# w_out on 128 and 32 lanes, row sums of two quarters, and a transposing lane maximum in a decode kernel of attention and gMLP

## The chip, the cores and the metric

The kernel runs on one core of one Trainium2 chip. The metric is the device time of one execution in microseconds, as the median of several runs. Every time below comes from these runs or from one profiled execution of the kernel before.

## The reference

One decode step (one token for each of four batch rows, D = 640) through two blocks that share a layer-normalized input. All inputs and the output are bfloat16.

```python
xn = layernorm(x)                                    # (4, 1, 640)
# A: 32 heads, Dh = 128, 4096 cached keys and values per batch row and head
q = (xn @ wq) per head
p = softmax(q . k_cache * 128**-0.5)                 # over the 4096 keys
a = (p . v_cache) @ wo                               # (4096, 640)
# B: gMLP, F = 1728, Fh = 864
z = gelu(xn @ w_in)
z1, z2 = z[..., :Fh], layernorm(z[..., Fh:])
g = w_sp * z2 + b_sp                                 # one token: two scalars
b = (z1 * g) @ w_out                                 # (864, 640)
out = x + a + b
```

k_cache and v_cache have 134 MB each; with wq, wo, w_in and w_out the kernel reads 282 MB from HBM.

## The kernel before

**Units.** The work goes by NU = 16 units: a unit is eight heads of one batch row (`hg, b = divmod(u, 4)`; HG = 4 groups of heads). Its keys, 8 MB, lie on 128 lanes, 16 lanes a head and 256 keys a lane, and are cut into NK = 4 quarters of 64 keys. The 64 quarters of all units are the steps `n` of the main loop (L708).

**A step.** `product` (L514, VectorE) multiplies the quarter by the query, which is broadcast to the lanes in `qbc`. `fold_half` (L520, VectorE) adds the upper half of the 128 columns to the lower. `sums` (L529, TensorE) adds the 64 columns that are left in eight groups of 8 by eight matmuls with the identity, into a PSUM tile `s_ps` of 64 x 8. `row_sums` (L542, VectorE) of the step before adds those eight into the scores `s_sb`.

**The end of a unit**, in the first step of the next one. `head_max` takes the maximum over a lane's 256 scores (L551), then over the 16 lanes of a head: a 32 x 32 transpose of that maximum, broadcast (L553), a mask `far` added (L556), a maximum with negation (L558). `exps` (L564, ScalarE) forms the exponentials and `by_head` (L575, VectorE) spreads them over the columns of their heads in one of two halves of the tile `p_m`. `stage_q` (L496, L504) makes `qbc` of the next unit.

**V.** In the second step of the next unit (`turns`, L697; the last units differ) `weighted` (L599) multiplies all of V by `p_m` with 64 matmuls into `pv`. `take` (L611, ScalarE) copies the result out and `pick_unit` (L630) collects it by head in `o_ps`.

**A group's turn.** After four units, in the first step of the unit after that (n = 20, 36, 52), `group_turn` divides by the denominators `den` (L640, L646), transposes (L655) and adds (L660), and `group_proj` (L668) multiplies by wo into `out_ps`. The matmul of `den` (`group_den`, L615) stands earlier, at the turn three steps before, ahead of `weighted`. The last group goes another way (L757 to L788): V of the last unit lies in the ring and is multiplied in pieces (L778) as they land.

**Order.** From L702 on the order on TensorE, VectorE, ScalarE and SP is the one written. The loads go out on SP's queue in the order of `loads` (L177). `pump` issues them as long as the place that the next one needs isn't in `busy`; K has a ring of seven quarters, V one place (`v_all`), and wo lies in a slot of the ring (`WO_AT`). A slot is given free as soon as its `sums`, its `weighted` or its `group_proj` are issued, and the DMA waits for their end.

**gMLP.** `gmlp` (L372) is a generator whose parts are run in steps 0 to 2. Its 864 columns are six chunks of 128 lanes and four of 24 (`NFF`, `FR`, `FT`): 100 matmuls form `zT` (L380), VectorE and ScalarE do gelu and layernorm, and 20 matmuls (L480) multiply by w_out. w_out lies in three parts: rows of six to a lane, of which five are in `v_all` and the sixth in the tile `p_m` (L118 to L121, by SP), and the last 96 rows on 24 lanes, also in `p_m`, by five transfers of five or four lanes each, issued by ScalarE (L115).

Of the kernel before, what the change touches and what calls it, by code (L numbers as in the profile page):

```python
# [9 lines left out]
FP32 = mybir.dt.float32  # L10
BF16 = mybir.dt.bfloat16
ACT = mybir.ActivationFunctionType
ALU = mybir.AluOpType
# [4 lines left out]
def kernel(  # L18
# [43 lines left out]
    NFF = Fh // P  # L62
    FR = 4
    FT = (Fh - NFF * P) // FR
    NFC = NFF + FR
    LS = 5
# [14 lines left out]
    once = ctx.enter_context(tc.tile_pool(name="once", bufs=1))  # L81
# [9 lines left out]
    p_m = const.tile([P, 2, NG, CB, HT], BF16, name="p_m")  # L91
# [12 lines left out]
    NV = NFF - 1  # L104
    at_v = -(-DC * (HD + F) // 256) * 256
    w_out_sb = v_all[:, at_v : at_v + NV * D].rearrange("p (k n) -> p k n", k=NV)
    p_w = p_m[:].rearrange("p n g c h -> p (n g c h)")
    at_p = -(-D // 256) * 256
    w_row_sb = p_w[:, 0:D]
    w_end_sb = p_w[:, at_p : at_p + FR * D].rearrange("p (r n) -> p r n", r=FR)  # L110
    nc.sync.dma_start(out=wq_sb, in_=A_wq.rearrange("(p c) n -> p c n", c=DC))

    w_end_rows = B_w_out[NFF * P : Fh].rearrange("(p r) n -> p r n", r=FR)
# [63 lines left out]
    loads = [k_load(0, 0, 2), (load_w, []), k_load(0, 2, 4), k_load(1)]  # L177
# [55 lines left out]
    nc.vector.memset(eps_tile[:], eps)  # L233
    ones_sq = const.tile([P, P], FP32)
    nc.vector.memset(ones_sq[:], 1.0)
# [39 lines left out]
    nc.vector.memset(xnT[:], 0.0)  # L275
# [32 lines left out]
    nc.vector.memset(pick[:], 0.0)  # L308
    nc.vector.tensor_copy(
# [29 lines left out]
    nc.vector.tensor_scalar(  # L339
# [31 lines left out]

    def gmlp():  # L372
        zz, gw, gt, gz = (gm[n] for n in ("zz", "gw", "gt", "gz"))
        zT = ps_pv.tile([P, 2, NFC, Bsz], FP32, tag="pv", name="zT")
        for t in range(2):
            f1 = t * Fh + NFF * P
            w_t = w_in_sb[:, :, t * Fh : f1].rearrange("p c (f k) -> p c k f", k=NFF)
            for k in range(NFC):
                for c in range(DC):
                    nc.tensor.matmul(  # L380
                        out=zT[: P if k < NFF else FT, t, k, :],
                        lhsT=w_t[:, c, k, :]
                        if k < NFF
                        else w_in_sb[:, c, f1 + k - NFF : f1 + FT * FR : FR],
                        rhs=xnT[:, c, 0:Bsz],
                        start=(c == 0),
                        stop=(c == DC - 1),
                    )
        yield
        nc.vector.tensor_copy(out=zz[:, :, 0:NFF, :], in_=zT[:, :, 0:NFF, :])  # L390
        nc.vector.tensor_copy(out=zz[:FT, :, NFF:], in_=zT[:FT, :, NFF:])
# [46 lines left out]
        nc.vector.tensor_copy(out=wsp_t[:], in_=wsp_bf[:])  # L438
        bsp_t = work.tile([1, 1], FP32, name="bsp_t")
        nc.vector.tensor_copy(out=bsp_t[:], in_=bsp_bf[:])  # L440
# [34 lines left out]
        w_terms = [w_out_sb[:, k] for k in range(NV)] + [w_row_sb]  # L475
        w_terms += [w_end_sb[:FT, r] for r in range(FR)]
        for k in range(NFC):
            w = P if k < NFF else FT
            for half in range(2):
                nc.tensor.matmul(  # L480
                    out=out_sum(half),
                    lhsT=gm["yT"][:w, k, :],
                    rhs=w_terms[k][:, half * NOH : (half + 1) * NOH],
                    start=False,
                    stop=False,
                )
# [37 lines left out]
    def sums(n):  # L524
        u, r, t = step(n)
        s = sums_ps[n] = ps_s.tile([P, HC, RW], FP32, name="s_ps")
        m = HD2 // RW
        for g in range(m):
            nc.tensor.matmul(  # L529
                out=s[:],  # L530
                lhsT=ident[:],
                rhs=t[:, :, g * RW : (g + 1) * RW],
                start=(g == 0),
                stop=(g == m - 1),
            )
        busy.remove(k_at[u][r])

    def row_sums(n):
        u, r, t = step(n)
        if n % NK == 0:  # L540
            scores[u] = small.tile([P, NR], FP32, name="s_sb")
        nc.vector.tensor_reduce(  # L542
            out=scores[u][:, r * HC : (r + 1) * HC],
            in_=sums_ps.pop(n)[:],
            axis=AX.X,
            op=ALU.add,
        )

    def head_max(u):
        m1 = small.tile([P, 1], FP32, name="m1")  # L550
        nc.vector.tensor_reduce(out=m1[:], in_=scores[u][:], axis=AX.X, op=ALU.max)  # L551
        mt = small.tile([P, PAR, LN], FP32, name="mt")
        nc.vector.transpose(  # L553
            out=mt[:].rearrange("p e l -> p (e l)"), in_=m1[:].to_broadcast([P, QD])
        )
        nc.vector.tensor_tensor(out=mt[:], in0=mt[:], in1=far[:], op=ALU.add)  # L556
        nm = small.tile([P, 1], FP32, name="nm")
        nc.vector.tensor_reduce(out=nm[:], in_=mt[:], axis=AX.XY, op=ALU.max, negate=True)  # L558
        maxes[u] = nm
# [78 lines left out]
    def group_turn(hg):  # L638
        rden = small.tile([P, 1], FP32, name="rden")
        nc.vector.reciprocal(out=rden[:], in_=rdens.pop(hg)[:])  # L640


        o_q = gr.pop(hg)[:].rearrange("p (q j) -> p q j", j=JR)
        o_n = once.tile([P, JR, PAR, QH], BF16, name="o_n")
        for e in range(PAR):
            nc.vector.scalar_tensor_tensor(  # L646
                out=o_n[:, :, e, :].rearrange("p j q -> p q j"),
                in0=o_q,
                scalar=rden[:, 0:1],
                in1=of_set[:, e : e + 1, None].to_broadcast([P, QH, JR]),  # L650
                op0=ALU.mult,
                op1=ALU.mult,
            )
        o_t = once.tile([P, JR, QD], BF16, name="o_t")
        nc.vector.transpose(  # L655
            out=o_t[:].rearrange("p j q -> p (j q)"),
            in_=o_n[:].rearrange("p j e q -> p (j e q)"),
        )
        o_s = once.tile([P, JR, Bsz], BF16, name="o_s")
        nc.vector.tensor_tensor(  # L660
            out=o_s[:], in0=o_t[:, :, 0:Bsz], in1=o_t[:, :, Bsz : 2 * Bsz], op=ALU.add
        )
        gr[hg] = [o_s[:, j, :] for j in range(JR)]
# [38 lines left out]
    with tc.manual_schedule(engines={E.PE, E.DVE, E.Activation, E.SP}):  # L702
# [5 lines left out]
        for n in range(NK * NU):  # L708
# [4 lines left out]
            if n:  # L713
                row_sums(n - 1)
# [110 lines left out]
```

## Time and profile before

| | us |
|---|---|
| runs of before | 662.22, 662.36, 663.16; median 662.36 |
| the profiled execution, from its first to its last instruction (the span) | 660.5 |
| busy: VectorE / TensorE / TensorE weight loads / ScalarE | 524.9 / 310.9 / 135.7 / 29.8 |
| VectorE idle before L514, for a landing of K | 86.3 |
| mean DMA rate over the span | 428 GB/s |
| granted TensorE clock, mean | 0.694 |

The profile has no other time of its execution than the span; the runs' median is 1.9 us longer. In the rows that follow PE is TensorE, PEld its weight loads, DVE VectorE, ACT ScalarE, POOL GpSimd and SP SyncE. A row of groups has the line, engine and operation, the output and input with their shapes, the count, then busy us, mean ns of one, and the idle time before them with its cause. A row of the chain or the timeline begins with its start and its length in us; times are from the start of the span. The row of digits is the busy share of 40 equal slices in tenths. q8 and q14 are queues that fetch instructions. Beside the views the trace holds a record of each DMA packet (start, length, size, queue) and the time at which each of 16 DMA engines reported its share of a transfer as landed; "packet records" and "landings" below are these.

### The profile page before, as it was taken

The page shows a single profiled execution, that of the slowest core. Times are in us where ns is not written, and L with a number is a line of the kernel's source. Part 1 is how long each engine was busy: PE and PEld are TensorE (multiplying, and loading weights), DVE is VectorE, ACT ScalarE, POOL GpSimd, SP SyncE. Part 2 cuts the span into 40 slices and gives each one's busy share as a digit, 9 for nine tenths or more (in the row PEclk, how much of TensorE's full clock was granted, in tenths as well). Part 3 has the DMA queues.
Part 4 walks back from the last instruction along what each step waited for, and adds up shares of the span by engine and source line. Part 5 has one row for each costly group of instructions (what it writes and reads, how often), then busy time and mean ns, then how long its engine had stood idle before and what let it go on. Part 6 is the DMA issues. An engine that isn't in the chain of part 4 may idle for free.

```text
span 660.5 us, 4704 instructions
## 1 busy us (share of the span) xinstructions
PE 310.9 (47%) x2035; PEld 135.7 (21%) x2035; DVE 524.9 (79%) x332; ACT 29.8 (5%) x73; POOL 2.7 (0%) x12
## 2 busy tenths in 40 slices
PE   0274363526527362472536336362462633736366
PEld 0131122212203121130212112121130221212124
DVE  2578988959598795969959598695969969999950
ACT  0020000000000000000000000000000000000000
POOL 1000000000000000000000000000000000000000
PEclk9756686766768677576767768677576767678765
DMA  9999999999999999999999999999999999999997
GB/s 372 435 448 429 430 441 437 438 425 437 430 433 438 433 433 438 433 434 425 437 437 438 421 433 438 441 438 433 429 426 441 430 433 445 411 428 437 457 400 281
DMA packets 8113, 282.56 MB, mean 428 GB/s; under 512 B 888, under 2 KB 2180, under 8 KB 2588
## 3 DMA queue, kind: packets, MB, share of 16 engines
q1 hardware_dynamic: 8024, 282.12, 99.0%
q8 instruction: 16, 0.26, 0.1%
q10 hardware_dynamic: 68, 0.13, 0.1%
q14 instruction: 5, 0.04, 0.0%
HBM read 282.24 MB, written 0.01 MB: 427 GB/s over the span
## 4 chain that ended last, share of the span: by engine, by line
DMA 60%; DVE 30%; PE 9%; issue 1%; ACT 0%; DVEq 0%; SPq 0%
DMA k_ring<-in_A_k_cache_dram 52%; DVE k_ring L514 15%; DVE k_ring L520 8%; PE s_ps L529 7%; DMA v_all<-in_A_v_cache_dram 4%; DMA k_ring<-in_A_wo_dram 3%; DVE s_sb L542 2%; DVE p_m L575 1%; DVE m L551 1%; PE out_ps L668 1%; DVE o_n L646 1%; PE zT L380 1%; PE pv L599 1%; DVE mt L553 0%; PE out_ps L480 0%
## 5 line engine op out<-in xcount | busy, mean ns | idle before, releaser
L514 DVE TENSOR_TENSOR k_ring<-k_ring,qbc 128x8192 bf16<-128x8192 bf16 x64 | 282.7, 4418 | 86.3 <-DMA k_ring<-in_A_k_cache_dram 86.3
L529 PE MATMUL s_ps<-k_ring,ident 128*128 128x512 bf16 x512 | 201.1, 564 | 313.7 <-DVE k_ring L520 313.5
L529 PEld LDWEIGHTS <-ident 128*128 128x128 bf16 x512 | 65.4, 129 | 427.7 <-issue 383.7
L520 DVE TENSOR_TENSOR k_ring<-k_ring 128x4096 bf16<-128x4096 bf16 x64 | 145.9, 2279 | 0.0
L599 PE MATMUL pv<-v_all,p_m 128*32 128x512 bf16 x960 | 60.2, 407 | 0.0
L542 DVE TENSOR_REDUCE s_sb<-s_ps 128x64 f32<-128x512 f32 x64 | 43.6, 682 | 5.7 <-PE s_ps L529 5.7
L575 DVE TENSOR_TENSOR p_m<-p_c,own 128x2048 bf16<-128x2048 bf16 x16 | 36.5, 2284 | 0.7 <-ACT p_c L564 0.7
L599 PEld LDWEIGHTS <-p_m 128*32 128x32 bf16 x992 | 25.8, 103 | 39.4 <-issue 17.1
L564 ACT ACTIVATE p_c<-s_sb,nm 128x256 bf16<-128x256 f32 x16 | 8.1, 508 | 331.2 <-DVE nm L558 331.2
L630 PEld LDWEIGHTS o_ps<-o_rows,pick 128*128 128x128 f32 x96 | 19.5, 280 | 4.1 <-issue 3.0
L630 PE MATMUL o_ps<-o_rows,pick 128*128 128x128 f32 x96 | 18.6, 357 | 0.0
L611 ACT COPY o_rows<-pv 128x512 f32<-128x512 f32 x16 | 9.4, 586 | 167.4 <-PE pv L599 167.4
L293 DVE TENSOR_SCALAR q_rows<-q_ps 128x512 bf16<-128x512 f32 x2 | 1.4, 692 | 12.3 <-PE q_ps L285 12.3
L786 DVE TENSOR_TENSOR o_n_last<-o_last,rden_all 128x32 bf16<-128x32 f32 x1 | 0.2, 192 | 12.3 <-PE o_last L778 12.3
L504 ACT CAST qbc<-qbc_ps 128x128 bf16<-128x128 f32 x16 | 4.3, 266 | 101.7 <-PE qbc_ps L496 101.7
L285 PE MATMUL q_ps<-v_all,xnT 128*32 128x512 bf16 x40 | 4.3, 618 | 8.9 <-DMA v_all<-in_A_wq_dram 8.9
L551 DVE TENSOR_REDUCE m<-s_sb 128x1 f32<-128x256 f32 x16 | 6.7, 420 | 0.6
L496 PE MATMUL qbc_ps<-q_rows,of_row 128*128 128x128 bf16 x32 | 6.0, 277 | 0.6 <-DVE q_rows L293 0.6
L496 PEld LDWEIGHTS <-of_row 128*128 128x128 bf16 x32 | 4.2, 134 | 8.3 <-issue 7.8
L668 PE MATMUL out_ps<-k_ring,o_s 128*4 128x320 bf16 x48 | 4.4, 331 | 2.2 <-DVE o_s L660 2.2
L685 PE MATMUL o_last<-hot,o_rows 128*128 128x8 f32 x32 | 4.9, 280 | 0.7 <-ACT o_rows L611 0.7
L685 PEld LDWEIGHTS o_last<-hot,o_rows 128*128 128x128 f32 x32 | 4.8, 225 | 1.8 <-ACT o_rows L611 1.6
(89 smaller groups left out, 74.6 us busy)
## 6 DMA issues: line engine op xcount, KB each, us to landing
k_ring<-in_A_k_cache_dram SPq DMA_DIRECT2D x6, 4096.0 KB, 24.8
v_all<-in_A_v_cache_dram SPq DMA_DIRECT2D x2, 4096.0 KB, 28.8
v_all<-in_A_wq_dram SPq DMA_DIRECT2D x1, 5120.0 KB
k_ring<-in_A_v_cache_dram SPq DMA_DIRECT2D x1, 4096.0 KB
k_ring<-in_A_wo_dram SPq DMA_DIRECT2D x3, 1280.0 KB, 20.1
v_all<-in_B_w_in_dram SPq DMA_DIRECT2D x1, 2160.0 KB
k_ring<-in_A_v_cache_dram SPq DMA_DIRECT2D x1, 2048.0 KB
k_ring<-in_A_v_cache_dram SPq DMA_DIRECT2D x1, 1024.0 KB
```

Of the source, the lines that this page charges most:

```text
L496: nc.tensor.matmul(out=qb_ps[:], lhsT=of_row[:, e, b].rearrange("p k f l -> p (k f l)"), rhs=q_rows[e][:, hg, :], start=(e == 0), stop=(e ...
L514: nc.vector.tensor_tensor(out=t, in0=t, in1=qbcs[u][:, None, :].to_broadcast([P, HC, Dh]), op=ALU.mult)
L520: nc.vector.tensor_tensor(out=t[:, :, 0:HD2], in0=t[:, :, 0:HD2], in1=t[:, :, HD2:Dh], op=ALU.add)
L529: nc.tensor.matmul(out=s[:], lhsT=ident[:], rhs=t[:, :, g * RW : (g + 1) * RW], start=(g == 0), stop=(g == m - 1),)
L542: nc.vector.tensor_reduce(out=scores[u][:, r * HC : (r + 1) * HC], in_=sums_ps.pop(n)[:], axis=AX.X, op=ALU.add,)
L551: nc.vector.tensor_reduce(out=m1[:], in_=scores[u][:], axis=AX.X, op=ALU.max)
L575: nc.vector.tensor_tensor(out=p_m[:, u % 2], in0=p_c.pop(u)[:].rearrange("p (g c) -> p g c", c=CB)[:, :, :, None].to_broadcast([P, NG, CB, HT]
L599: nc.tensor.matmul(out=pvs[u][cg * QD : (cg + 1) * QD, :], lhsT=p_m[:, u % 2, g0 + n].rearrange("p c h -> p (c h)"), rhs=v_at[:, n * CB : ...
L611: nc.scalar.copy(out=o[:].rearrange("p c d -> p (c d)"), in_=pvs.pop(u)[:])
L630: nc.tensor.matmul(out=gr[hg][:], lhsT=pick[:, c, Bsz - 1 - b : P + Bsz - 1 - b], rhs=o[:, c, :], start=(b == 0 and c == 0), stop=(b == Bs ...
L668: nc.tensor.matmul(out=out_sum(half), lhsT=o, rhs=wo_sb[:, n, half * NOH : (half + 1) * NOH], start=False, stop=(hg == HG - 1 and n == HT ...
L685: nc.tensor.matmul(out=o_last[0][:, :, :, u % Bsz], lhsT=o[:, c, :], rhs=hot[:, c, :].rearrange("p (k e) -> p k e", e=PAR), start=(c == 0) ...
```

## The change

Four things are changed together.

1. w_out: 640 rows lie five to a lane on 128 lanes (`w_a_sb`, in `v_all`), and 224 rows seven to a lane on 32 lanes (`w_b_sb`). The second part is read by four transfers of eight lanes each (lanes l, l + 4, ...), on SP's queue, after the first half of K of unit 0 and before w_in. gMLP has five chunks of 128 lanes and seven of 32: 120 matmuls for `zT`, 24 for the product with w_out.
2. `sums` of two successive quarters share a PSUM tile of two banks, and `row_sums` runs once for both, in even steps. To make room, `ps_pv` and `ps_m` have one buffer in place of two, and `group_den` is issued in `group_turn`.
3. `head_max`: the lane maximum is added to `far` as a scalar for each lane, and one reduce with `apply_transpose` takes the maximum over the lanes. Three operations in place of four.
4. Eight small operations of the head go from VectorE to GpSimd. The tiles of `group_turn` move into the tile `p_m` behind its two halves (`p_end`), which w_b covers at first as well.

```diff
-    ps_pv = ctx.enter_context(tc.tile_pool(name="ps_pv", bufs=2, space=PSUM))
-    ps_m = ctx.enter_context(tc.tile_pool(name="ps_m", bufs=2, space=PSUM))
+    ps_pv = ctx.enter_context(tc.tile_pool(name="ps_pv", bufs=1, space=PSUM))
+    ps_m = ctx.enter_context(tc.tile_pool(name="ps_m", bufs=1, space=PSUM))
...
+    FA, FL, LS = 5, 32, 4
+    FB = (Fh - FA * P) // FL
+    NFC = FA + FB
...
-    for l in range(LS):
-        nc.scalar.dma_start(out=w_end_sb[l:FT:LS], in_=w_end_rows[l:FT:LS])
+    def load_w_b():
+        for l in range(LS):
+            nc.sync.dma_start(out=w_b_sb[l:FL:LS], in_=w_b_rows[l:FL:LS])
     def load_w():
         nc.sync.dma_start(out=w_in_sb, in_=B_w_in.rearrange("(p c) n -> p c n", c=DC))
-        w_rows = B_w_out[0 : NFF * P].rearrange("(p k) n -> p k n", k=NFF)
-        nc.sync.dma_start(out=w_out_sb, in_=w_rows[:, 0:NV])
-        nc.sync.dma_start(out=w_row_sb, in_=w_rows[:, NV])
+        nc.sync.dma_start(
+            out=w_a_sb, in_=B_w_out[0 : FA * P].rearrange("(p k) n -> p k n", k=FA)
+        )
...
-    loads = [k_load(0, 0, 2), (load_w, []), k_load(0, 2, 4), k_load(1)]
+    loads = [k_load(0, 0, 2), (load_w_b, []), (load_w, []), k_load(0, 2, 4), k_load(1)]
...
     def sums(n):
         u, r, t = step(n)
-        s = sums_ps[n] = ps_s.tile([P, HC, RW], FP32, name="s_ps")
+        if n % 2 == 0:
+            sums_ps[n // 2] = ps_s.tile([P, 2, HC, RW], FP32, name="s_ps")
+        i = n % NK // 2 * 2
+        s = sums_ps[n // 2][:, sorted(k_order[u][i : i + 2]).index(r)]
...
     def row_sums(n):
-        u, r, t = step(n)
-        if n % NK == 0:
+        u, i = divmod(n, NK)
+        if i == 1:
             scores[u] = small.tile([P, NR], FP32, name="s_sb")
+        lo, hi = sorted(k_order[u][i - 1 : i + 1])
         nc.vector.tensor_reduce(
-            out=scores[u][:, r * HC : (r + 1) * HC],
-            in_=sums_ps.pop(n)[:],
+            out=scores[u][:].rearrange("p (r c) -> p r c", r=NK)[:, lo : hi + 1 : hi - lo],
+            in_=sums_ps.pop(n // 2)[:],
...
     def head_max(u):
         m1 = small.tile([P, 1], FP32, name="m1")
         nc.vector.tensor_reduce(out=m1[:], in_=scores[u][:], axis=AX.X, op=ALU.max)
-        mt = small.tile([P, PAR, LN], FP32, name="mt")
-        nc.vector.transpose(
-            out=mt[:].rearrange("p e l -> p (e l)"), in_=m1[:].to_broadcast([P, QD])
-        )
-        nc.vector.tensor_tensor(out=mt[:], in0=mt[:], in1=far[:], op=ALU.add)
+        mf = small.tile([P, QD], FP32, name="mf")
+        nc.vector.tensor_scalar(
+            out=mf[:],
+            in0=far[:].rearrange("p e l -> p (e l)"),
+            scalar1=m1[:, 0:1],
+            scalar2=None,
+            op0=ALU.add,
+        )
         nm = small.tile([P, 1], FP32, name="nm")
-        nc.vector.tensor_reduce(out=nm[:], in_=mt[:], axis=AX.XY, op=ALU.max, negate=True)
+        nc.vector.tensor_reduce(
+            out=nm[:], in_=mf[:], axis=AX.X, op=ALU.max, apply_transpose=True, negate=True
+        )
...
     def group_turn(hg):
+        group_den(hg)
         rden = small.tile([P, 1], FP32, name="rden")
...
-            if n:
+            if n and n % 2 == 0:
                 row_sums(n - 1)
...
             if n in turns:
                 w = waiting = turns[n]
-                if w % Bsz == Bsz - 1:
-                    group_den(w // Bsz)
```

The operations that go to GpSimd are the fills of `eps_tile`, `ones_sq`, `xnT` and `pick`, the copy into `pick`, the forming of `far`, and the copies `wsp_t` and `bsp_t`.

More of the change, by code (lines that the diff above doesn't have):

```diff
@@ L370, with lanes @@
     gm["yT"] = work.tile([P, NFC, Bsz], BF16, name="yT")
+    def lanes(k):
+        return P if k < FA else FL
     def gmlp():
@@ L375, in gmlp @@
         for t in range(2):
-            f1 = t * Fh + NFF * P
-            w_t = w_in_sb[:, :, t * Fh : f1].rearrange("p c (f k) -> p c k f", k=NFF)
+            w_t = w_in_sb[:, :, t * Fh : (t + 1) * Fh]
             for k in range(NFC):
+                w_k = (
+                    w_t[:, :, k : FA * P : FA]
+                    if k < FA
+                    else w_t[:, :, FA * P + k - FA : Fh : FB]
+                )
                 for c in range(DC):
                     nc.tensor.matmul(
[L381 to L384, printed above, removed]
+                        out=zT[0 : lanes(k), t, k, :],
+                        lhsT=w_k[:, c],
                         rhs=xnT[:, c, 0:Bsz],
@@ L529, in sums @@
             nc.tensor.matmul(
-                out=s[:],
+                out=s,
                 lhsT=ident[:],
```

60 lines of the change are left out of this document (26 added, 34 removed).

## The prediction

> **What bounds the kernel now.** I read the page first, then the groups by form, the chain of waits, the timeline of the group turn and of the tail, and last the packet and landing records of the trace.
>
> ```profile
> PE 310.9 (47%) x2035; PEld 135.7 (21%) x2035; DVE 524.9 (79%) x332; ACT 29.8 (5%) x73; POOL 2.7 (0%) x12
> ...
> DVE  2578988959598795969959598695969969999950
> ...
> DMA  9999999999999999999999999999999999999997
> ...
> q8 instruction: 16, 0.26, 0.1%
> ...
> q14 instruction: 5, 0.04, 0.0%
> ```
>
> VectorE is busy 79% and is idle mostly while it waits for K (86.3 us before L514). The DMA row is full in 39 of 40 slices. In the packet records no engine has a gap from 16 us to 653 us: eight 64 KB packets take 19.30 us between two landings, unit after unit. So the time is the byte stream of the *slowest* of 16 DMA engines, plus a tail. The chain ends in it:
>
> ```profile
> 600.84 3.53 PE s_ps L529 x8
> 604.36 3.60 PE pv L599 x64
> 607.98 26.36 DMA v_all<-in_A_v_cache_dram
> 634.36 21.95 DMA k_ring<-in_A_wo_dram
> 656.35 1.30 PE out_ps L668 x8
> ```
>
> The engines do not end together. The last piece of wo lands on eight of them at 653.73 to 655.26 and on the other eight at 656.42 to 657.17. The landings show how that grows: the spread is 1.3 us at 33 us, and each of the 16 KB code fetches (q8, 16 of them) sets one engine back by 1.43 us (0.93 us itself, 0.5 us on the next packet). They go round the same eight engines in turn. Seven of these, hit twice, are seven of the late eight; the eighth late one took three 8 KB fetches (q14). The five engines that carried the five-lane packets (5120 B, 196 ns each) are not among the eight that fetch.
>
> The Trainium skill (Runtime: NRT & Kernel Launch, Instruction fetch mechanics) calls a block crossing mostly hidden. Here it is hidden from TensorE, not from the DMA stream: 1.43 us each.
>
> **The change part by part.** The profiled span is 660.5 us, the median of the runs 662.36: 1.9 us lie around the span, and I leave them as they are.
>
> *w_out's loads.* Bytes are the same. Removed: the 1280 B row (8 packets of 55 ns per engine; its landing comes 0.39 us after the one before it) and the five-lane packets, 0.205 us each with their completion, five on four engines and four on a fifth. Added: four transfers of eight lanes, 8960 B a lane. Between 6400 B (244 ns) and 10240 B (385 ns) that is 0.338 us, 0.347 us with completion, so 1.39 us. Five-lane transfers ran on five engines, so I take eight lanes on eight. Balance: four engines 1.39 - 1.03 - 0.39 = -0.03 us, one 1.39 - 0.82 - 0.39 = +0.18, three 1.39 - 0.39 = +1.00, eight -0.39. Which eight get nothing? If the late eight, the end moves by -0.39; if a late one is among the three, by +1.00. I take the first, because the five known ones are not among those that fetch code; the three then end by 655.26 + 1.00 = 656.3, still ahead of 657.17 - 0.39 = 656.8.
>
> The Trainium skill (DMA: Bandwidth & Descriptors, Why a DMA increments its semaphore by 16 and not by 1) says that such a transfer runs on the lowest-numbered k engines, k being the largest divisor up to 16. The five packets per five-lane transfer agree; by it eight lanes fall on engines 0 to 7, which would put the fetches on 8 to 15.
>
> The loads move from ScalarE's queue to SP's, ahead of w_in, w_a and the rest of K. Five issues on ScalarE (3.59 us) go; its first table load waits behind them until 4.94 us, but q_ps waits for wq until 16.45 us: 0. Four more issues on SP at 0.33 to 0.42 us: the bytes ahead of K of unit 1 last until 41.8 us, where its predecessor begins to land, and it is issued at 36.5: 0. If a completion semaphore is reused late, SP waits for the first half of K at 26.0 us while 5 us of w_in are still queued: 0.
>
> *GMLP.* Twelve chunks for ten: 20 more matmuls of zT at 42 ns (0.84 us; VectorE waits for them) and 4 of L480 (about 0.6 us). V's first load goes at 56.92 us while K's landing begins at 61.09; K of unit 2 at 76.58, V's landing at 80.43. Both may slip by over 2 us: 0. The 48 further TensorE instructions bring code fetches forward, none is added: the sixteenth came at 4048 of 4078.
>
> *Row sums and maximum.*
>
> ```profile
> L542 DVE TENSOR_REDUCE s_sb<-s_ps 128x64 f32<-128x512 f32 x64 | 43.6, 682 | 5.7 <-PE s_ps L529 5.7
> ...
> L553 DVE STREAM_TRANSPOSE mt<-m 128x32 f32<-128x32 f32 x16 | 3.4, 211 | 0.5
> ...
> L556 DVE TENSOR_TENSOR mt<-mt,far 128x32 f32<-128x32 f32 x16 | 3.1, 192 | 0.6
> ...
> L558 DVE TENSOR_REDUCE nm<-mt 128x1 f32<-128x32 f32 x16 | 3.0, 186 | 0.5
> ```
>
> One row sum takes 0.604 us of the chain. A double one lies between 1.137 (twice, less one overhead of 0.07) and 1.364 (2 x 682); I take 1.137, as the elements dominate. That is -0.07 us a pair, 32 pairs: -2.2 us. In the maximum three steps of 0.24 + 0.23 + 0.18 us become two. The transposing reduce lies between 0.186 (L558) and 0.40 (L553 + L558); I take 0.2, nearer the plain reduce, since the elements are as few: -0.2 us a unit, -3.2 in all. Some 5.4 us of VectorE, but hidden: it waits for K anyway until 534 us. The diff also puts eight small head operations on POOL, in the 16 us before wq lands: 0.
>
> *One PSUM buffer for pv and m.* q_rows come about 1 us later (0.69 us copy between two sets of matmuls), at 22.5 us against K at 26.1: 0. pv is emptied in the same step or the next unit's first, before the next use: 0. But den (L615) moves from the turn into group_turn:
>
> ```profile
> 228.52 0.16 DVE L640 RECIPROCAL rden<-den 128x1 f32<-128x1 f32 x1
> 228.80 1.33 DVE L646 SCALAR_TENSOR_TENSOR o_n<-o_ps,rden,of_set 128x128 bf16<-128x128 f32 x2
> 229.82 0.42 PE L496 MATMUL qbc_ps<-q_rows,of_row 128*128 128x128 bf16 x2
> ...
> 230.33 0.27 ACT L504 CAST qbc<-qbc_ps 128x128 bf16<-128x128 f32 x1 [5.43 <-PE qbc_ps L496]
> ```
>
> VectorE's reciprocal, which waits for nothing now, will wait for sums, qbc, ScalarE's copy (230.60) and two passes of den (0.7 us): until 231.35, a stall of 2.8 us at steps 20, 36 and 52. Behind it are o_n, the next product, out_ps and, through the slot of wo, the next K load: 232.76 becomes about 236.0, first packet 0.95 us later, 237.0; the first engine runs dry at 237.9. Step 36 is alike (394.6 against 395.5). Cover about 1 us; without it the early engines idle first, and the late ones end 2 us and more behind them: 0.
>
> From step 52 VectorE runs without a pause to 632.7. It carries 2.8 us in, gains 6 x 0.07 + 3 x 0.2 = 1.0, so 1.8 us late; the last row sum is double (+0.5), the last maximum shorter (-0.2). by_head ends at 641.2 + 2.1 = 643.3. weighted(15), which waits for V until 644.04, comes at 645.1 behind the picks; its 1.07 us are eaten by the waits after it (0.41, 0.24 and 0.65 us before the L778 groups). The end is still wo's landing.
>
> Sum: -0.39 us on the late engines, +0.1 for small slips: 660.5 - 0.3 + 1.9 = 662.1; I say 662.0 us.
>
> **Rivals.** *The tail turns VectorE-bound (slower).* The place is steps 52 to the last by_head; it decides from 2.4 us late, and I have 2.1. At the upper prices, 1.364 for seven pairs (+1.6) and 0.40 for four maxima (+0.8), it is 4.5 us late, 2.1 too much: 662.0 + 2.1 = 664.1. For it: no spare time after 645 us. Against: each price at its end. 0.20.
>
> *The loaded engines are late ones.* +1.0 us in place of -0.39: 662.36 + 1.0 = 663.4. Only landing order speaks against it. If code fetches did not decide the order, as the skill's runtime page would have it, this is what would come. 0.12.
>
> *VectorE's 5.4 us reach the end (faster).* 662.36 - 5.4 = 657.0 if the chain were VectorE's throughout. Against: a DMA stream without a gap; evening out the sixteen engines could give no more than half of their spread of 3.4 us, 660.6. 0.06.
>
> *The changed instructions save nothing* (the reduce is built as two): VectorE's time is hidden, 662.2. 0.06.
>
> **How the numbers follow.** My forecast has 0.56, at 662.0. A change of 0.2% (1.3 us) is about what a measurement of this kernel can tell from no change. Slower by more: three quarters of the first rival (0.15) and some of the second (0.03), 0.18. Faster by more: the third and a little of the forecast, 0.07. The rest, 0.75, lies within. The range runs from 661.2 (the forecast less the 0.9 us by which the three runs of before differ, rounded) to 664.2 (the first rival).
>
> **What would show it.** Right: the DMA row still full, span near 660.2; two groups of eight engines in the landings, closer by 0.4 us or more; q14 with four fetches, as VectorE's third comes at its 312th of 360 instructions and would have no place; L640 idle about 2.8 us before each of three, on PE den; pv at 645 behind the picks. Wrong: idle time of PE before the last out_ps that names a VectorE step, a DMA slice under 9 near 232, 390 or 608 us, K's first landing clearly after 26 us, a transposing reduce over 0.4 us.

## The result: 664.97 us, slower by 0.33%

The changed kernel takes 664.97 us (median of 5 runs, 663.21 to 665.52); the kernel before took 662.36 us beside it. The ratio is 1.0033, with a 95% interval of 1.0022 to 1.0044: 2.6 us slower, where 662.0 us was forecast and 664.2 us was the upper end. The profiled run took 664.97 us and its span is 663.2 us, against 660.5 us before. In what follows, the times of a kernel are medians of all its runs; landings, issues and packets come from its one profiled run.

The rows of the changed kernel's page that answer to those of before (busy time, tenths in 40 slices, queues):

```profile
PE 317.6 (48%) x2059; PEld 135.6 (20%) x2059; DVE 522.4 (79%) x276; ACT 29.9 (5%) x73; POOL 6.2 (1%) x20
...
DVE  1569978959597696969969589795959869999960
...
DMA  9999999999999999999999999999999999999996
...
q8 instruction: 16, 0.26, 0.1%
...
q14 instruction: 4, 0.03, 0.0%
```

By the page nothing has happened: VectorE has 56 rows fewer and is busy 2.5 us less, and the DMA row is still full in 39 slices. A slice is 16.6 us long, so a hole of half a microsecond on each engine cannot be seen in it. The end of the chain of waits of the changed kernel names what stands at the end:

```profile
601.29 2.30 DVE k_ring L523
603.64 3.57 PE s_ps L535 x8
607.21 4.77 PE pv L611 x34
612.00 23.22 DMA v_all<-in_A_v_cache_dram
635.24 23.43 DMA k_ring<-in_A_wo_dram
658.70 1.53 PE out_ps L680 x8
660.25 0.42 ACT res L802
```

The bound is the same as before: the last piece of wo, on the slowest DMA engine. It lands at 659.75 us on that engine instead of 657.17 (+2.58), while the mean over the sixteen engines is +1.66. So the engines lost time somewhere, and the slowest lost more than the mean. The landings of each transfer, compared with the same transfer of before, show where (K(u) and V(u) are the loads of unit u):

```
landing of                   mean of 16 engines   last engine     (after - before, us)
w_out (at 33 us)                  -0.25              -0.12
K of unit 1 (62 us)               -0.10              +0.85
V of unit 0 (81 us)               +0.62              +0.55
K at 139 us                       +0.63              +0.46
last half of K (613 us)           +0.83              +0.69
V of unit 14 (633 us)             +1.42              +0.88
next landing (647 us)             +1.53              +2.40
last piece of wo (656 us)         +1.66              +2.58
```

The mean jumps twice, by 0.72 at V(0) and by 0.59 at V(14), and lies between 0.58 and 0.87 from one to the other. The packet records show the reason at both places. V(0) is issued at 58.66 us, and the first engines finish K(1) at 60.32; 14 of the first packets of V(0), one of them behind a code fetch, then take 2.62 to 3.87 us instead of 2.418, 10.0 engine-us more in all (engine-us: summed over the sixteen engines). V(14) is issued at 612.00, the first engines are empty at 612.31, the first packet starts at 612.97, and nine packets are stretched by 5.1 engine-us, beside 5.6 engine-us of idle engines. Before, V(0) was issued at 56.92 and V(14) at 607.98, and none of the first packets was stretched.

Why V(0) is late, in the timeline of before (first three lines) and of the changed kernel:

```profile
36.50 4.22 PE L380 MATMUL zT<-xnT,v_all 128*128 128x4 bf16 x100
...
40.83 0.21 DVE L390 COPY zz<-zT 128x48 f32<-128x48 f32 x1 [3.63 <-PE zT L380]
...
56.92 0.33 SPq L157 DMA_DIRECT2D v_all<-in_A_v_cache_dram  x1
```

```profile
36.17 6.15 PE L387 MATMUL zT<-xnT,v_all 128*128 128x4 bf16 x120
...
42.43 0.20 DVE L395 COPY zz<-zT 128x40 f32<-128x40 f32 x1 [5.51 <-PE zT L387]
...
58.66 0.33 SPq L157 DMA_DIRECT2D v_all<-in_A_v_cache_dram  x1
```

The 20 matmuls more cost 1.93 us, not 0.84, and VectorE hands that on, step by step, to the issue of V(0). And why V(14) is late: the denominator, in the changed kernel's timeline of the group turn at step 52,

```profile
547.31 0.42 PE L499 MATMUL qbc_ps<-q_rows,of_row 128*128 128x128 bf16 x2
547.82 0.27 ACT L507 CAST qbc<-qbc_ps 128x128 bf16<-128x128 f32 x1 [5.43 <-PE qbc_ps L499]
548.14 0.38 PE L627 MATMUL den<-ones_sq,acc 128*128 128x1 f32 x2 [0.41 <-ACT qbc L507]
548.56 0.17 DVE L653 RECIPROCAL rden<-den 128x1 f32<-128x1 f32 x1 [2.49 <-PE den L627]
```

After this stall VectorE is 3.3 us behind the kernel before (550.70 against 547.41 at the next product), and 2.8 us at its last fold ahead of V(14) (601.29 against 598.51). A slower weighted(14), 4.80 us instead of 3.64, adds 1.2 us. The row by stretches of time, of the changed kernel and of before, gives the granted TensorE clock in its third column from the end:

```profile
607.00:612.00 5.00, 4.95 (x65) 1.82 (x64) 4.90 (x6) 0.60 (x2) 0.00 (x0) 0.74 0.97 419
```

```profile
604.00:608.00 4.00, 3.93 (x65) 1.70 (x65) 3.86 (x7) 0.62 (x3) 0.00 (x0) 0.98 1.04 451
```

The jump of the last engine at 647 us is of another kind. At 648.23 us the fifteenth TensorE code fetch runs, and from the landing at 643 us to the next one, the latest of the sixteen goes from 644.96 to 651.29, the second latest from 644.93 to 649.82. The fetch met an engine that was among the last already, and it lands last from there on. Before, the fifteenth fetch (647.9 us) moved an engine that had 1.9 us in hand.

### The profile page after: what moved, and what is told of

Its sections match the earlier page's. It is cut to its first block, busy times and chain, and to the rows that moved or that the text cites. A ratio compares the mean times of both kernels' runs of the same rounds, so it can differ in the third digit from the quotient of the medians.

```text
span 663.2 us, 4721 instructions
## 1 busy us (share of the span) xinstructions
PE 317.6 (48%) x2059; PEld 135.6 (20%) x2059; DVE 522.4 (79%) x276; ACT 29.9 (5%) x73; POOL 6.2 (1%) x20
## 4 chain that ended last, share of the span: by engine, by line
DMA 62%; DVE 27%; PE 10%; issue 1%; ACT 0%; SPq 0%; DVEq 0%; ACTq 0%
DMA k_ring<-in_A_k_cache_dram 55%; DVE k_ring L517 14%; PE s_ps L535 8%; DVE k_ring L523 7%; DMA k_ring<-in_A_wo_dram 4%; DMA v_all<-in_A_v_cache_dram 4%; DVE s_sb L549 3%; PE out_ps L680 1%; DVE m L558 1%; PE pv L611 1%; DVE p_m L659 1%; DVE mf L560 1%; DVE nm L568 0%; DVE p_m L587 0%; PE den L627 0%
## 5 line engine op out<-in xcount | busy, mean ns | idle before, releaser
L535 PEld LDWEIGHTS <-ident 128*128 128x128 bf16 x512 | 63.6, 130 | 417.4 <-issue 239.7
L611 PE MATMUL pv<-v_all,p_m 128*32 128x512 bf16 x960 | 62.6, 420 | 0.0
L549 DVE TENSOR_REDUCE s_sb<-s_ps 128x128 f32<-128x1024 f32 x32 | 39.0, 1218 | 3.7 <-PE s_ps L535 3.7
L623 ACT COPY o_rows<-pv 128x512 f32<-128x512 f32 x16 | 9.4, 586 | 165.8 <-PE pv L611 165.7
L680 PE MATMUL out_ps<-k_ring,p_m 128*4 128x320 bf16 x48 | 6.3, 433 | 6.9 <-DVE p_m L672 6.9
L387 PE MATMUL zT<-xnT,v_all 128*32 128x4 bf16 (+1 forms) x120 | 6.2, 187 | 0.0
```

Source lines behind the costliest of these rows:

```text
L535: nc.tensor.matmul(out=s, lhsT=ident[:], rhs=t[:, :, g * RW : (g + 1) * RW], start=(g == 0), stop=(g == m - 1),)
L549: nc.vector.tensor_reduce(out=scores[u][:].rearrange("p (r c) -> p r c", r=NK)[:, lo : hi + 1 : hi - lo], in_=sums_ps.pop(n // 2)[:], axis ...
L611: nc.tensor.matmul(out=pvs[u][cg * QD : (cg + 1) * QD, :], lhsT=p_m[:, u % 2, g0 + n].rearrange("p c h -> p (c h)"), rhs=v_at[:, n * CB : ...
L623: nc.scalar.copy(out=o[:].rearrange("p c d -> p (c d)"), in_=pvs.pop(u)[:])
L680: nc.tensor.matmul(out=out_sum(half), lhsT=o, rhs=wo_sb[:, n, half * NOH : (half + 1) * NOH], start=False, stop=(hg == HG - 1 and n == HT ...
```

## The experiments: the two halves undone

Theory A: the loss is the two places where the queue runs dry. Theory B: it is the place of w_out's loads. Theory C: VectorE's lateness in the tail. The first four kernels undo the parts one at a time and together.

**Denominator early** (w_out part kept):

```
 turn:        + if w % Bsz == Bsz - 1: group_den(w // Bsz)
 step 4(u+1): + group_rden(waiting // Bsz)        # reciprocal, ahead of head_max
 group_turn:  - group_den(hg); rden = ...         # uses the rden taken above
```

> The changed kernel with one thing undone: the group's denominator is computed where it was before the change, in the turn (step 4(u+1)+1), and its reciprocal is taken at the head of the next group's first step, so that the one PSUM buffer is free again for q's broadcast. Theory A (the queue ran dry): the three stalls of 2.2 to 2.7 us at L653 go, V(14) is issued near 609.4 instead of 612.00, two us and more before the first engines run dry at 612.4, so the 5.6 engine-us of idle at 612 to 616 go, the engines keep their distances and the code fetch near 648 falls on an engine that has room: about 663.5 us (663.0 to 664.2). Theory B (the loaded engines decide: w_out's eight-lane transfers and the code fetches at the head make the late ones later): nothing at the end changes, 664.8 to 665.2. Theory C (the tail hangs on VectorE): the whole 2.5 us come back, 662.5 or less.

Measured: 663.42 us (663.22 to 664.00; ratio 1.0018, 1.0009 to 1.0027). The stalls are gone (L652 has no idle time before it), weighted(14) takes 3.77 us, V(14) is issued at 608.31, and no packet is stretched at 612 us. V(0) is stretched still (14 packets by 6.5 engine-us). Theory A's number was 663.5.

**w_out as before, denominator late:**

```
-FA, FL, LS = 5, 32, 4      +NFF, FR, LS = 6, 4, 5    # six chunks of 128, four of 24 lanes
-sync: 4 x w_b[l::4], w_a   +scalar: 5 x w_end[l::5]; sync: w_out, w_row
```

> The changed kernel with w_out loaded and multiplied as before the change (six chunks of 128 lanes and four of 24, five transfers of five lanes on the ScalarE queue); the rest of the change stays. Theory A: zT takes 4.2 us again, V(0) is issued near 57 instead of 58.66, and the 3.4 engine-us of idle at 61 us go; the second gap at 612 stays: about 664.2 us (663.9 to 664.5). Theory B: the whole loss goes with the loads, 662.5 to 663.2. Theory C: no change, 664.8 to 665.2.

Measured: 662.36 us (ratio 1.0008, 0.9998 to 1.0018). V(0) is issued at 56.91 and nothing is stretched at 61 us; V(14) is issued at 611.30, and five packets are stretched by 3.3 engine-us. Theory A said 664.2: it had the places right and the price of the second one wrong, and theory B's 662.5 to 663.2 comes nearer to this time. In the profiled run (662.36 us) the mean of the last landing is 0.69 late and the last engine only 0.10: the engines that stood idle were not the last ones, and no fetch met the last one afterwards. But the eleven runs reach from 661.76 to 665.41, three of them over 663.6, where 130 of the 133 runs of the kernel before lie from 662.0 to 663.0 and the other three at 663.16, 663.27 and 663.97. The price of this gap seems to vary from run to run.

**Both:**

> Both edits together: w_out as before the change and the denominator early. What is left of the change is the row sums of two quarters at once, the lane maximum that transposes, the POOL moves and the single PSUM buffers. Theory A: neither gap, 662.4 us (662.0 to 662.9), the time of the kernel before. Theory B: the same as the kernel with the old w_out alone (within 0.3). Theory C: 662.5 or less.

Measured: 662.07 us (ratio 0.9995, 0.9987 to 1.0004), without either gap. Its profiled run is one that began its transfers 1.2 us late and is not used for landings. What is left of the change (row sums of two quarters, transposing maximum, POOL moves, single buffers) makes no difference that can be measured, as forecast.

**w_out alone in the kernel before:**

> The kernel before with only the w_out part of the change (eight-lane transfers, 5 chunks of 128 lanes and 7 of 32, the buffers that it needs); row sums, lane maximum, denominator and PSUM buffers as before. Theory A: V(0) is issued late (58.3 to 58.9) and the queue runs dry there, but V(14) is in time: 662.36 + 0.75 = 663.1 us (662.7 to 663.5). Theory B: the whole loss, 664.5 to 665.2. If the four relieved engines were the late ones: 662.0.

Measured: 663.56 us (ratio 1.0018, 1.0009 to 1.0027), V(0) issued at 58.63, 15 packets stretched by 8.5 engine-us. (In its profiled run weighted(14) was slow too, 4.73 us; V(14) went out at 610.31 and four packets were stretched by 1.9 engine-us.) The time is 0.14 from the first kernel, which has all of the VectorE savings: they are worth nothing here. Theory C falls with it.

The four corners: 664.97 (new w_out, late denominator), 663.42, 662.36, 662.07. The late denominator costs 1.55 us with the new w_out and 0.29 with the old one, which is within the noise; the w_out part costs 2.61 and 1.35. They do not add, and the w_out part costs more than theory A's 0.75.

## The gap at V(0) taken away by itself

The ring slot of K(2)'s second quarter is free after step 1. Loading it ahead of V(0) gives the queue 4.8 us more of work and changes no computation:

```
 loads after k_load(1):  + k_load(2, 1, 2)
 for u = 0:  v_load(0), - k_load(2)   + k_load(2, 0, 1), k_load(2, 2, 4)
```

> The kernel with the denominator early (663.42 us), and one change in the order of the transfers: the second quarter of K(2), whose ring slot is free after step 1, is loaded before V(0), and the rest of K(2) in two transfers behind it. V(0) is still issued near 58.6, but the queue has 4.8 us more of work then. The w_out part, its late zT and the second TensorE code fetch at 61 us stay. Theory A (the dry queue at V(0) costs the time): no stretched packets at 60 to 63 us, the head's gain of 0.34 us shows at the end, 661.9 us (661.5 to 662.5). Theory F (the code fetch that the 48 new TensorE instructions pull from 78 to 61 us, and the engines that w_out's eight-lane transfers load): no change, 663.2 to 663.7.

> The changed kernel with the early quarter of K(2) alone; the denominator stays late. Theory A: the gap at V(0) goes and the one at V(14) stays, as in the kernel with the old w_out: a median of 662.0 to 663.3 us with single runs up to 2 us above it, because then it depends on which engine the last two code fetches meet. Theory F: 664.8 to 665.2.

> The kernel with the old w_out and the denominator early (662.07 us), with the early quarter of K(2). V(0) is in time there anyway, so the quarter has nothing to cover. Both theories: 661.9 to 662.3 us. If it is faster by more, the order of the loads is worth something by itself, and the gain of the early quarter in the other kernels is not that of the gap.

Measured: 662.66 us (662.47 to 662.84; ratio 1.0004), 663.33 us (662.50 to 665.15; 1.0019) and 662.30 us (661.98 to 663.22; 1.0001). V(0) is still issued late in the first, but behind work:

```profile
26.42 24.40 SPq L146 DMA_DIRECT2D k_ring<-in_A_k_cache_dram  x3
58.56 0.33 SPq L157 DMA_DIRECT2D v_all<-in_A_v_cache_dram  x1
```

No packet is stretched there. The quarter takes 1.64 us from the changed kernel and 0.76 from the one with the early denominator, and costs 0.23 where there was no gap, which is within the noise. So the gap at V(0) is worth 0.8 to 1.0 us (0.76, or 0.76 + 0.23) with the early denominator and 1.6 to 1.9 with the late one. The prediction of 661.9 was missed by 0.8, though: the mean of the last landing is 0.20 early against the kernel before, the last engine 0.39 late. That is not theory F (no change) and not all of theory A.

The second of the three shows one more thing. Its denominator is late, but in its profiled run (662.59 us, near the low end of its eleven) weighted(14) took 3.64 us, V(14) went out at 610.14 and no packet was stretched there. In the first, with the early denominator, weighted(14) took 4.78 us and V(14) went out at 609.19. So the 1.2 us of a slow weighted(14) come and go whether the denominator is late or not, and the gap at V(14) was widest where they came on top of the late denominator. What lowers the granted clock there is not shown.

The opposite test makes the gap in the kernel before:

```
 gmlp, after zT:  + the chunks 0 to 7 of t = 1 once more (40 matmuls, same place)
```

> The kernel before, with 40 of zT's 100 matmuls done twice (the second time into the same place, so that the values stay), and nothing else: w_out's loads, the VectorE instructions and the buffers are those of before. 40 matmuls of 42 ns are 1.7 us, so V(0) is issued near 58.6 instead of 56.92, as in the changed kernel. Theory A: the packets of V(0) are stretched at 60 to 63 us by 6 to 10 engine-us, and the kernel takes 662.33 + 0.8 to 1.2 = 663.1 to 663.5 us. Theory that w_out's loads decide: 662.2 to 662.5.

```profile
36.43 4.22 PE L380 MATMUL zT<-xnT,v_all 128*128 128x4 bf16 x100
40.58 1.90 PE L391 MATMUL zT<-xnT,v_all 128*128 128x4 bf16 x40
```

Measured: V(0) is issued at 58.69, 11 packets are stretched by 5.9 engine-us, and the time is 662.95 us (ratio 1.0009, 1.0000 to 1.0018), +0.65 with w_out's loads untouched. The runs are of two kinds, five at 662.35 to 662.58 and six at 662.95 to 663.70. The forecast of 0.8 to 1.2 holds for the second kind alone; the profiled run (662.52) is of the first, with the mean of the last landing 0.37 late and the last engine 0.14.

## What is left of the w_out part

Without gaps the new w_out still costs 0.36 us (662.66 against 662.30), which the intervals of the two ratios (0.9995 to 1.0013, 0.9992 to 1.0009) do not separate; in the profiled runs its last landing comes 0.66 us later (657.56 against 656.90). Its sixteen last landings are

```
653.67 654.11 654.44 654.80 654.95 655.09 655.31 655.94 655.97 656.00 656.05 656.08 656.09 656.11 657.13 657.56
```

Fourteen end by 656.11, 1.1 us earlier than the last one of before, and two stand alone. Which engines are these? Five kernels moved the load of the 32-lane part (`LS` is the number of its transfers), the first three with `LS = 2`:

> The kernel with the denominator early and the early quarter of K(2) (662.66 us), with the 32-lane part of w_out in two transfers of sixteen lanes instead of four of eight. A lane's 8960 B take 0.347 us with the completion: the engines that took four of them (1.39 us) take two (0.69 us), and the other engines get 0.69 us that they did not have. No gap is in this kernel, so only the place of the load changes. Theory L (the engines that w_out's eight lanes load are among those that take the code fetches, so they end last): -0.69, 662.0 us (661.8 to 662.3). Theory N (the late engines are those that the eight-lane transfers spared, as the prediction took them): +0.69, 663.3 us. If the place does not matter: 662.5 to 662.8.

> The changed kernel (664.97 us) with the 32-lane part of w_out in two transfers of sixteen lanes, and nothing else; zT stays long, the denominator stays late, so both gaps stay. Theory L: 664.3 us, with single runs over 2 us apart. Theory N: 665.6. If the load's place were the whole of the loss, and the gaps nothing: 662.3.

> The kernel with the denominator early (663.42 us; the gap at V(0) stays, the one at V(14) is gone) with two transfers of sixteen lanes. Theory L: 662.7 us. Theory N: 664.1. If the gap's price and the load's place add up, the four kernels with and without the early quarter, with eight and with sixteen lanes, differ by the same amounts (0.76 for the gap).

Measured: 663.18, 665.11 and 663.51 us (ratios 1.0012, 1.0040, 1.0018). Neither theory: the edit did not do what I meant. The sixteen-lane packets took 0.34 to 0.67 us, and those of w_in behind them 0.64 to 1.34 instead of 0.644, so all sixteen engines were set back, in the first kernel by 0.8 us on average against the kernel before. That its time is near theory N's 663.3 comes from this delay. The lone pair is gone (the late eight lie within 0.5 us), but the time cannot tell why.

```
 LS = 8 (four lanes each)
```

> The kernel without gaps (denominator early, early quarter of K(2), eight-lane transfers: 662.66 us) with the 32-lane part of w_out in eight transfers of four lanes. Four engines then carry eight lanes each (2.78 us instead of 1.39) and four carry none (-1.39). In the kernel without gaps fourteen engines land by 656.11 and two alone at 657.13 and 657.56. Theory L2 (two of the engines that carry eight-lane packets also take code fetches; these are the two): they come down to 655.7 and 656.2, the four with the double load stay below 656.8, and the time is 661.5 to 662.0 us. Theory N (the two late ones are engines that carry none of it): 662.6 us or more, with the four loaded ones behind them or not.

```
 LS = 2, and load_w_b behind load_w
```

> The kernel without gaps with two transfers of sixteen lanes (663.18 us), which now come behind w_in and the 128-lane part instead of ahead of them. Ahead of them the packets of w_in (17280 B) took 0.65 to 1.29 us, which set all sixteen engines back by 1.0 us, while the two late engines were gone from the landings. If that stretch is a matter of the order: every engine gains 0.8 to 1.0, the two late ones do not come back, 661.9 to 662.3 us. If it belongs to sixteen-lane transfers wherever they are: 663.0 to 663.4.

Measured: 667.08 us and 663.06 us (ratios 1.0071, 1.0013). The first is a miss of its own kind. SyncE came through its eight issues only at 27.7 us, so w_in came late and everything behind it:

```profile
1.63 26.06 SPq L115 DMA_DIRECT2D p_m<-in_B_w_out_dram  x8
27.73 0.44 SPq L118 DMA_DIRECT2D v_all<-in_B_w_in_dram  x1
```

The second says that sixteen-lane packets are stretched wherever they stand (0.34 to 0.66 us), here without harm to w_in. So the load was left out altogether, and with it a part of the sum; the kernel serves for this question alone:

```
 load_w_b:  - 4 transfers   + nc.gpsimd.memset(w_b_sb, 0.0)
```

> The kernel without gaps (denominator early, early quarter of K(2): 662.66 us) in which the 32-lane part of w_out isn't loaded: GpSimd writes zeros in its place, so that 287 KB of w_out are left out of the sum, and every instruction that computes stays. Half of the engines then lose four packets of 8960 B, 1.39 us each; the others lose nothing. Theory L2 (the two engines that land last, at 657.13 and 657.56, carry these packets): both come down by 1.39, the last landing is near 656.2 and the time 661.2 to 661.7 us. Theory N (the last two are engines that carry none): the last landing stays at 657.5 and the time at 662.5 to 662.8.

Measured: 661.69 us (661.60 to 661.94; ratio 0.9988, 0.9979 to 0.9997), and these last landings:

```
653.23 653.27 653.44 653.60 653.75 653.75 654.19 654.88 654.90 655.98 656.01 656.03 656.04 656.06 656.07 656.32
```

Six engines are where they were, 655.98 to 656.07 against 655.97 to 656.11: they carry none of the load, and they are late through code fetches. The pair at 657.13 and 657.56 is gone: nothing lands after 656.32, so the last landing has come down by 1.24 us and each of the two by 0.8 at least, as theory L2 said. So two of the eight engines that carry w_out's eight-lane packets also take code fetches, and the new loads put them behind all others.

The landings of the kernel without gaps, followed from one transfer to the next, agree. Behind w_out's loads they form an early and a late group, and the late one holds the eight engines with the load. Six of the first eight fetches set back an engine of the early group. The other two, at 109.8 and 165.8 us, set back one of the late group. The first of these stands apart from its neighbours by about 0.1 us and more, so that it can be followed to the end: it lands at 100.52 us in one transfer, falls 1.56 us behind at the fetch of 109.8 us and 1.55 at that of 482.0, and is the engine that lands at 657.13. For the one at 657.56 the landings around 165.8 us lie too close together to be sure.

The Trainium skill (DMA: Bandwidth & Descriptors, Why a DMA increments its semaphore by 16 and not by 1) puts a transfer of eight lanes on the eight lowest-numbered engines; eight loaded and eight spared agrees with the landings here, but that the fetches use only the spared ones, as I took it, does not.

The last kernel put the load on the five engines of the old five-lane transfers:

```
 LS = 7, nc.sync -> nc.scalar     # four transfers of five lanes, three of four
```

> The kernel without gaps, with the 32-lane part of w_out in seven transfers of five and four lanes on ScalarE's queue, where the five-lane transfers of the kernel before were. Four engines then carry seven packets of 8960 B (2.43 us instead of 1.39), one carries four, three carry none (-1.39). The run without the load has shown that two of the eight loaded engines take code fetches and end last; in the kernel before, the five engines that five-lane transfers use were not among the late eight. If the two are among the three that are spared now: they come down to 656.2 or less, the four others rise from 655.3 at most to 656.3, the last landing is 656.1 to 656.5 and the time 661.3 to 661.9 us, faster than the kernel before. If one of them is among the five: 662.7 us or more.

```profile
1.35 16.39 ACTq L115 DMA_DIRECT2D p_m<-in_B_w_out_dram  x7
17.83 1.28 ACT L253 ACT_TABLE_LOAD   x1 [17.83 <-DMA v_all<-in_A_wq_dram]
```

Measured: 664.48 us (ratio 1.0032). ScalarE stood at its seventh issue until wq had landed, and its square root for the layer norm came at 19.13 us. K's second half went out at 21.41 us, 5 us earlier than in the kernel without gaps, but the packets of wq, K(0) and w_in took 26 engine-us longer than there, and the mean of the last landing is 1.9 us later. What stretched them, and whether those five engines would have been the right ones, stays open. No complete version beat the kernel before beyond doubt; the one with the old w_out and the early denominator (662.07, 0.9995, 0.9987 to 1.0004) is level with it and 2.9 us faster than the changed one.

## Why the prediction was wrong, by its own steps

- **The bound** was right: the stream of the slowest engine plus a tail, before and after. The first rival's place (from step 52 on) was right and its mechanism was not: VectorE's lateness did not reach the end through a chain of VectorE work, but by issuing V(14) too late for the queue. The third rival's condition did not come; the fourth's (the reduce built as two) did not either, though the changed instructions saved next to nothing for another reason, given below. The sign named for a dry queue, a DMA slice under 9, did not show, since such a gap is too short for a slice.
- **"Both may slip by over 2 us: 0"** is the step that failed first. Its slip was mis-sized: 0.84 us for zT, measured 1.93. The rows by form, of the changed kernel and of before, show the part of it:

```profile
L387 PEld LDWEIGHTS <-v_all 128*32 128x32 bf16 x70 | 3.9, 150 | 0.0
```

```profile
L380 PEld LDWEIGHTS <-v_all 128*24 128x24 bf16 x40 | 1.1, 100 | 0.0
```

  A weight load of 32 lanes, taken from w_in with a stride of 7, is 150 ns, one of 24 lanes with a stride of 4 is 100, though the granted clock in this stretch was 0.77 against 0.50 before. And its reserve, the time that an issue has before an engine runs out of packets, was read from the wrong event: it compared the issue with the landing at 61.09 us, but the first engine runs out when its own packets end, at 60.3. V(0) went from 3.84 us of reserve to 1.66, and that was not enough.
- **"First packet 0.95 us later"**, taken from the head where the queues are empty, was the term behind it. It held where engines stood empty: 0.97 us at V(14) (612.00 to 612.97). At V(0) the first packet starts 1.93 us after its issue. What the term leaves out are the stretched packets: all sixteen engines run at 2.418 us a packet only 5.4 us after the issue of V(0). Over all the profiles, a reserve of 2.5 us and more gave no stretched packet. From 1.9 to 2.5 us it gave from none (609.19 us in the kernel without gaps, 1.9 us) to 6.0 engine-us (the longer zT, 2.1 us, where all engines end within 2.2 us of each other); 1.8 us and less gave from 0.1 (532.95 us with w_out alone, ahead of packets of half the size) to 10. The Trainium skill (DMA: Bandwidth & Descriptors, Specifications) has 0.6 us to the first byte on this path. Counted from the end of the issuing instruction (0.33 us), the 0.97 us at V(14) are 0.64, which agrees.
- **"Early engines idle first, late ones end 2 us and more behind them: 0"** failed in the size of a chance, not in the mechanism. At the small gap at 236 us (three packets stretched by 2.9 engine-us, the mean 0.18 later and the last engine not at all), and in the profiled runs of the old w_out and of the longer zT, it is what happened (last engine +0.10 and +0.14 while the mean is +0.69 and +0.37). At 394 us one packet was stretched, by 0.5 us. But the engines' distances are what the later code fetches, 1.4 us each, are absorbed by. After a gap the sixteen stand closer together, and a fetch can meet the last one, as at 648.23 us. That this makes the spread of the runs with a gap (up to 3.7 us) is argued from one profiled run, not shown for the others.
- **den** was right in place and close in size, 2.22, 2.70 and 2.49 us for 2.8. What was not followed was V(14): the tail was taken as 1.8 us late, the issue of V(14) was 4.0 late, 2.8 from VectorE and 1.2 from weighted(14) at a granted clock of 0.74. The 1.0 us that VectorE was to gain behind step 52 came to 0.15 (3.29 us late at 550.70, 3.14 at 614.33). The early denominator gives 1.55 us back.
- **w_out's loads.** The mean of the sixteen engines came 0.25 us early at 33 us, where the balance of the prediction adds up to nothing (four times -0.03, once +0.18, three times +1.00 and eight times -0.39 give -0.06 us for all sixteen). "I take the first" failed: two late engines were among the loaded, as the second rival said, and its 1.0 us is about what the pair stands behind; it costs about 0.36 us of time by the medians, since the other engines were relieved.
- **Row sums and maximum.** The instructions were right: a double row sum takes 1.13 us of the chain (1.137 forecast, with an overhead of 0.07 that no row shows by itself), the transposing reduce 0.21 (0.2). The saving was not. The start of a product, two steps apart, in the kernel before and in the changed one:

```profile
579.30 4.42 DVE L514 TENSOR_TENSOR k_ring<-k_ring,qbc 128x8192 bf16<-128x8192 bf16 x1
593.57 4.42 DVE L514 TENSOR_TENSOR k_ring<-k_ring,qbc 128x8192 bf16<-128x8192 bf16 x1
```

```profile
582.51 4.42 DVE L517 TENSOR_TENSOR k_ring<-k_ring,qbc 128x8192 bf16<-128x8192 bf16 x1
596.84 4.42 DVE L517 TENSOR_TENSOR k_ring<-k_ring,qbc 128x8192 bf16<-128x8192 bf16 x1
```

  A pair of steps takes 14.33 us where it took 14.27: +0.06, not -0.07. A row sum starts 4.34 us after its product, but in the step that has none now the fold starts 4.45 us after it (601.29 against 596.84). A whole unit, maximum included, takes 31.82 us instead of 31.89, so VectorE gains about 1.1 us in sixteen units, not 5.4. None of it reaches the end. No code fetch was added (16), and q14 has four, as said.
- A slip without consequence: 662.0 less 0.9 is 661.1, not the 661.2 of the range.

The loss of 2.6 us, put together by undoing: the late denominator 1.55, the gap at V(0) 0.76 after that, 0.36 for the pair of engines (against the same order of loads with the old w_out). The sum, 2.67, depends on the order of undoing, and its last term is within the noise.

## What to carry to other kernels

Where a stream of transfers is the bound, the reserve of an issue is counted from the issue to the moment the *first* engine ends its *last packet*, and some 2.5 us of it were needed here, not the latency of an idle queue. A page whose DMA row is all nines hides holes of half a microsecond: compare landings, mean and last of the engines, transfer by transfer. And a load that uses half of the engines is judged by which other traffic those engines have, code fetches included.

## What the runs showed of the hardware that I had not expected

- A transfer issued 1.7 us before the queue runs dry begins nearly in time (first packet 1.93 us after the issue), but its first 64 KB packets take up to 3.87 us instead of 2.418. The loss shows as slow packets more than as idle engines.
- Sixteen-lane transfers of one 8960 B packet per engine were stretched from 0.338 to as much as 0.67 us; eight-lane ones took 0.338 each.
- Seven or eight small transfers in a row on one queue held up their issuing engine until earlier large ones had landed. SyncE issued its fifth at 15.98 us and its sixth at 25.62, just behind the landings of wq (15.97) and of the first half of K(0) (25.60), and came free at 27.7; ScalarE came free at 17.7.
- The second TensorE code fetch came at 60.3 to 64.5 us in every kernel with a longer zT, and at 76.6 to 77.9 in the others. The order in which the eight engines take the fetches begins at another engine from one profile to the next: the two of them that carry w_out's load were the first two in the changed kernel, the third and fourth in the kernel without gaps.
